# Moving the q and k transposes from TensorE to crossbar DMA, with VectorE copies from SBUF

## The chip, the cores and the metric

The kernel runs on one core of one Trainium2 chip. The metric is the device time of that core in microseconds (us); lower is better. Executions of one kernel mostly lie within 1% of each other; where they scatter more, the text says so. A run counts as slow when it is over 1.5% above the fastest of the same kernel.

Five engines work side by side: PE (TensorE, matmul), DVE (VectorE), ACT (ScalarE), POOL (GpSimd) and SP (SyncE, which here only issues DMAs). Each works through its own list of instructions in a fixed order and stops at the first one whose input is not there (below, VectorE stands 10.43 us before one copy while the input of a later one is ready).

## The reference, cut to what matters

Attention over 8 batches of 8 heads (576 positions, head size 64) with a bias made of running sums, then a mixer: a low-rank mix along the sequence, and a channel mix 512 → 2048 → 512.

```python
cum = np.cumsum(np.maximum(s, 0.0), axis=-1)
bias = -(cum[:, :, :, None] - cum[:, :, None, :])
scores = np.where(causal, -1e9, scale * q @ k.T + np.minimum(bias, 0.0))
attn = softmax(scores);  x = (attn @ v)            # 8 x 576 x 512 after the heads are joined
u = x + (x.T @ U @ V).T                            # sequence mix
out = u + np.maximum(u @ w_ch1, 0.0) @ w_ch2       # channel mix
```

## The kernel before

Heads are handled two at a time: 32 head pairs, numbered n, four to a batch. The score matmuls of this kernel take q and k with the head dimension on the partitions, so each pair's q and k are transposed and copied into one of five "slots" (pair n uses slot n % 5). The transposes run on PE, 16 a pair, into PSUM; VectorE (ScalarE for a few early ones) copies PSUM to the slot.

```python
    def transposes(n):
        b, hp = divmod(n, PB)
        slot = slots[n % NSLOT]
        # ... SP fetches the four bias rows of the slot (cut)
        for hh in range(2):
            h = 2 * hp + hh
            tp = pwork().bitcast(BF16)[:, : 2 * 4 * TP].rearrange("p (c t m) -> p c t m", c=2, t=4)
            for c, src in enumerate((q_t[b], k_t[b])):
                for t2 in range(4):
                    nc.tensor.transpose(
                        tp[:, c, t2, :], src[:, h, ds(t2 * 128, 128)], identity[:TP, :TP]
                    )
            dst = slot[0:D, hh, 0 : 2 * S].rearrange("p (c m t two) -> p c m t two", c=2, t=4, two=2)
            for par in range(2):
                copy = nc.scalar.copy if n == 0 or (b == 1 and par) else nc.vector.tensor_copy
                copy(
                    dst[:, :, :, :, par],
                    tp[par * D : par * D + D].rearrange("p c t m -> p c m t"),
                )
            yield
```

The main loop runs two batches' loads ahead and fills the gaps of the attention with channel-mix matmuls of earlier groups (`step_fill`, inside `run`):

```python
    load(2)
    # ... (cut)
    for n in range(PB, NP + 2):
        b, hp = divmod(n, PB)
        if hp == 0 and 1 < b < B - 1:
            load(b + 1)
        if n + 1 < NP:
            run(transposes(n + 1))
        if n < NP:
            run(scores(n))
        # ... values(n - 1), seqmix(b - 1), chanmix (cut)
    in_program_order(tc, traced, [E.Pool, E.PE])
```

The order of the instructions on each engine is chosen when the kernel is compiled. `in_program_order` adds an edge from each instruction of an engine to the one before it in the program, and so keeps that engine in program order. For the whole program only Pool and PE are held like this. VectorE, ScalarE and SP are held only through batch 0 and are ordered freely by the compiler's scheduler from there on.

The softmax here doesn't subtract the row's maximum and nothing guards it: scores larger than these inputs give would overflow.

## Time and profile before

| | before |
|---|---|
| median time | 404.22 us (3 runs, 404.01 to 404.5) |
| profiled span | 400.4 us, mean granted TensorE clock 0.983 |
| PE busy | 381.6 us (95%) |
| DVE / ACT / POOL busy | 223.8 / 200.5 / 56.6 us |

The page of the kernel before, cut to the busy times and four rows of the picture in 40 slices. A digit is the busy share of a slice (10 us) in tenths; PEclk is the granted TensorE clock in tenths; DMA is the mean busy share of the 16 DMA engines.

```profile
span 400.4 us, 8275 instructions
...
PE 381.6 (95%) x3395; PEld 213.8 (53%) x3395; DVE 223.8 (56%) x473; ACT 200.5 (50%) x384; POOL 56.6 (14%) x79
...
PE   7798989989999899999999999999999999999995
...
DVE  7775036777567866776676756775668252002011
...
PEclk9759999999999999999999999999999999999999
DMA  5999999994596299319951792240154015301002
```

PE is busy 80% or more in every slice from the third to the 39th (most digits are 9), and VectorE has slack in every slice. DMA is full in slices 2 to 9: batch 2's q and k are loaded there, behind weights and the loads of earlier batches.

What does a PE transpose cost? The timeline of PE in the kernel before, around 198 us (columns: start, duration, engine, line, operation, tiles, shapes, count).

```profile
197.94 1.03 PE L432 MATMUL pwork<-uT,w_sb 128*128 128x512 bf16 x4
198.81 0.29 PE L237 MATMUL pwork<-identity,q_sd 72*128 72x72 bf16 x4
198.94 0.29 PE L237 MATMUL pwork<-identity,k_sd 72*128 72x72 bf16 x4
199.07 1.03 PE L432 MATMUL pwork<-uT,w_sb 128*128 128x512 bf16 x4
```

The eight transposes of one head start at 198.81 and the next matmul starts at 199.07, so a group of eight costs 0.26 us of PE's time, two groups 0.52 us a pair. The durations overlap and must not be added.

The groups by shape of VectorE in the kernel before: one slot's copies out of PSUM, and the one cast from SBUF to SBUF of the same shape (busy us, mean ns of one, idle time before).

```profile
L243 DVE COPY slot_93<-pwork 64x576 bf16<-64x576 bf16 x26 | 20.7, 798 | 2.2 <-PE pwork L237 1.9
...
L159 DVE CAST hT<-hT 64x576 bf16<-64x576 f32 x1 | 0.5, 453 | 0.0
```

### The profile page before, as it was taken

The numbers are of one execution on the slowest core, as the hardware profiler recorded it, in microseconds if no ns is written. First come the engines' busy times: TensorE is split into PE (matmuls) and PEld (weight loads), VectorE is DVE, ScalarE is ACT, GpSimd is POOL, SyncE is SP. The second block draws the span as 40 slices with busy tenths as digits, with TensorE's granted clock in tenths as the row PEclk, the third lists the DMA queues.
The fourth block names the chain that finished last, engine by engine and source line by source line (L and its number), as shares of the span: only waits on it lengthen the run. The fifth ranks groups of instructions, "written<-read, shape, count | busy, mean of one in ns | idle before, by whom it ended". The sixth has DMA issues, their size and how long they took to land.

```text
span 400.4 us, 8275 instructions
## 1 busy us (share of the span) xinstructions
PE 381.6 (95%) x3395; PEld 213.8 (53%) x3395; DVE 223.8 (56%) x473; ACT 200.5 (50%) x384; POOL 56.6 (14%) x79
## 2 busy tenths in 40 slices
PE   7798989989999899999999999999999999999995
PEld 2475446645655455555554566555555554444442
DVE  7775036777567866776676756775668252002011
ACT  5552578735753477336743584348533920630610
POOL 5760052300500050005000500000000000000000
PEclk9759999999999999999999999999999999999999
DMA  5999999994596299319951792240154015301002
GB/s 76 160 213 207 166 121 141 137 146 85 82 133 86 67 148 120 55 56 175 114 67 57 141 145 54 72 97 18 38 77 97 16 34 133 79 26 71 10 26 79
DMA packets 94148, 38.31 MB, mean 96 GB/s; under 512 B 77150, under 2 KB 88446, under 8 KB 94110
## 3 DMA queue, kind: packets, MB, share of 16 engines
q0 software_dynamic: 53360, 18.44, 57.5%
q1 hardware_dynamic: 40750, 19.35, 24.1%
q8 instruction: 26, 0.43, 0.5%
q14 instruction: 12, 0.10, 0.1%
HBM read 37.51 MB, written 9.95 MB: 119 GB/s over the span
## 4 chain that ended last, share of the span: by engine, by line
PE 76%; DMA 11%; DVE 6%; ACT 3%; issue 1%; POOL 1%; DVEq 0%; ACTq 0%
PE pwork L444 28%; PE pwork L432 28%; PE pscore L258 8%; DMA k_sd<-in_k_dram 8%; PE pwork L321 6%; PE pwork L237 3%; DMA v_slot_102<-in_v_dram 2%; PE pwork L349 2%; PE pwork L385 2%; DVE slot_96 L243 1%; DVE slot_95 L243 1%; DMA hT<-in_s_dram 1%; DVE x_sb L331 1%; DVE ux L357 1%; DVE o_sb L454 1%
## 5 line engine op out<-in xcount | busy, mean ns | idle before, releaser
L439 ACT ACTIVATE hT<-pwork 128x512 bf16<-128x512 f32 x144 | 88.0, 611 | 112.5 <-PE pwork L432 111.6
L444 PE MATMUL pwork<-w_sb,hT 128*128 128x512 bf16 x576 | 141.3, 379 | 0.2 <-ACT slot_96 L243 0.2
L432 PE MATMUL pwork<-uT,w_sb 128*128 128x512 bf16 x576 | 141.0, 379 | 0.4 <-ACT slot_96 L243 0.3
L444 PEld LDWEIGHTS <-hT 128*128 128x128 bf16 x576 | 52.3, 98 | 50.1 <-issue 0.3
L432 PEld LDWEIGHTS <-w_sb 128*128 128x128 bf16 x576 | 51.0, 98 | 46.9 <-issue 0.4
L454 DVE TENSOR_TENSOR o_sb<-pwork,u_sd 128x512 f32<-128x512 f32 x36 | 24.9, 692 | 63.4 <-PE pwork L444 62.2
L269 ACT ACTIVATE pT_87<-pscore 128x512 bf16<-128x512 f32 x32 | 19.3, 604 | 28.3 <-PE pscore L258 28.2
L331 DVE TENSOR_TENSOR x_sb<-pwork,rec 128x320 bf16<-128x320 f32 x64 | 31.3, 490 | 2.0
L98 POOL DMA_DIRECT2D q_sd<-in_q_dram x10 | 8.3, 829 | 148.6 <-PE pwork L237 132.5
L269 ACT ACTIVATE pT_86<-pscore 128x512 bf16<-128x512 f32 x32 | 19.3, 604 | 18.5 <-PE pscore L258 18.4
L243 DVE COPY slot_96<-pwork 64x576 bf16<-64x576 bf16 x22 | 17.4, 797 | 13.8 <-PE pwork L237 13.5
L270 DVE TENSOR_TENSOR pT_86<-pT_86,keep 128x512 bf16<-128x512 bf16 x32 | 13.2, 414 | 21.1 <-ACT pT_86 L269 21.0
L330 DVE RECIPROCAL rec<-pwork 128x5 f32<-128x5 f32 x64 | 12.1, 191 | 20.8 <-PE pwork L321 20.7
L367 DVE TENSOR_TENSOR uT<-pwork,xT 128x256 bf16<-128x256 f32 (+6 forms) x54 | 19.8, 418 | 6.1 <-PE pwork L385 6.1
L270 DVE TENSOR_TENSOR pT_87<-pT_87,keep 128x512 bf16<-128x512 bf16 x32 | 13.2, 417 | 17.5 <-ACT pT_87 L269 17.4
L237 PEld LDWEIGHTS <-q_sd 72*128 72x128 bf16 x256 | 15.9, 100 | 12.8 <-DMA q_sd<-in_q_dram 1.6
L237 PE MATMUL pwork<-identity,k_sd 72*128 72x72 bf16 x256 | 19.1, 201 | 2.9 <-DMA k_sd<-in_k_dram 2.8
L243 DVE COPY slot_93<-pwork 64x576 bf16<-64x576 bf16 x26 | 20.7, 798 | 2.2 <-PE pwork L237 1.9
L282 ACT ACTIVATE pT_87<-pscore 128x512 bf16<-128x512 f32 x32 | 19.5, 610 | 4.6 <-PE pscore L258 4.5
L282 ACT ACTIVATE pT_86<-pscore 128x512 bf16<-128x512 f32 x32 | 19.5, 609 | 4.5 <-PE pscore L258 4.5
L321 PEld LDWEIGHTS <-pT_87 128*128 128x128 bf16 x480 | 18.6, 99 | 5.8 <-DVE pT_87 L295 0.4
L321 PEld LDWEIGHTS <-pT_86 128*128 128x128 bf16 x480 | 18.4, 100 | 4.8 <-DVE uT L367 0.5
(96 smaller groups left out, 434.1 us busy)
## 6 DMA issues: line engine op xcount, KB each, us to landing
out_dram<-o_sb SPq DMA_DIRECT2D x36, 256.0 KB
w_sb<-in_moe_w_ch_dram POOLq DMA_DIRECT2D x2, 2048.0 KB, 20.6
q_sd<-in_q_dram POOLq DMA_DIRECT2D x7, 576.0 KB, 8.1
k_sd<-in_k_dram POOLq DMA_DIRECT2D x7, 576.0 KB, 14.0
v_slot_102<-in_v_dram POOLq DMA_DIRECT2D x12, 128.0 KB, 14.3
v_slot_103<-in_v_dram POOLq DMA_DIRECT2D x12, 128.0 KB, 14.7
v_slot_104<-in_v_dram POOLq DMA_DIRECT2D x8, 128.0 KB, 16.9
rows_hbm<-hT SPq DMA_DIRECT2D x1, 504.0 KB
```

What stands on the lines that cost most here:

```text
L237: nc.tensor.transpose(tp[:, c, t2, :], src[:, h, ds(t2 * 128, 128)], identity[:TP, :TP])
L243: copy(dst[:, :, :, :, par], tp[par * D : par * D + D].rearrange("p c t m -> p c m t"),)
L258: nc.tensor.matmul(dst, lhsT=kT[:, ds(j * 128, 128)], rhs=qT[:, lo:hi], start=True, stop=True,)
L269: nc.scalar.activation(pT[:, hh, 0:512], diag, EXP, scale=scale)
L270: nc.vector.tensor_tensor(pT[:, hh, 0:512].rearrange("p (a b) -> p a b", a=4), pT[:, hh, 0:512].rearrange("p (a b) -> p a b", a=4), keep.t ...
L282: nc.scalar.activation(pT[:, hh, 512:1024], far, EXP, scale=scale)
L321: nc.tensor.matmul(po[:, i, :], lhsT=pT[:, hh, ds(place(j, i), 128)], rhs=vt[:, j, h, :], start=(j == 0), stop=(j == i), skip_group_check= ...
L331: nc.vector.tensor_tensor(x_sb[:, hp, :, ds(hh * D, D)], po[:, :, 0:D], rec.to_broadcast([128, 5, D]), op=ALU.mult,)
L432: nc.tensor.matmul(f1, lhsT=w1_sb[:, kt, ds(nf * 128, 128)], rhs=u[:, kt, :], start=(kt == 0), stop=(kt == 3),)
L439: nc.scalar.activation(hT[:, nf, :], f1, RELU)
L444: nc.tensor.matmul(f2, lhsT=hT[:, nf, ds(i * 128, 128)], rhs=w2_sb[:, nf, :], start=(nf == 0), stop=(nf == NF - 1),)
L454: nc.vector.tensor_tensor(o_sb.rearrange("p (a b) -> p a b", a=4), f2.rearrange("p (a b) -> p a b", a=4), u_sd[:, :, i, :], op=ALU.add,)
```

## The change

The intent: PE is the limit, so take work off PE. For the pairs from 8 on (batches 2 to 7) a DMA that transposes in the crossbar writes q and k of a pair, transposed, to SBUF. VectorE copies from there to the slot. The loads now share one tile `qk` of 80 rows (72 used) per batch, two tiles in turn; Pool clears rows 64 to 79 before the first load that is read by the crossbar.

```diff
+    TR = 80
+    qks = [consts.tile([TR, H, 2, TT * D], BF16, name=f"qk{i}") for i in range(2)]
 ...
+    def fetch(n):
+        b, hp = divmod(n, PB)
+        qkT_of[n] = work.tile([128, 2, 2, 4, TR], BF16, tag="qkT", name="qkT")
+        nc.sync.dma_start_transpose(
+            out=qkT_of[n].rearrange("p a c t m -> p (a c t) m"),
+            in_=qks[b % 2][:, ds(2 * hp, 2), :, :].rearrange("p h c x -> p (h c x)"),
+        )
 
     def transposes(n):
 ...
+        qkT = qkT_of.pop(n, None)
         for hh in range(2):
+            if qkT is not None:
+                tp = qkT[:, hh, :, :, :TP]
+            else:
+                tp = pwork()...          # the eight PE transposes as before (cut)
 ...
     def load(b):
-        alloc_qk(b)
+        if b < FT + 2:
+            nc.gpsimd.memset(qks[b % 2][64:, :, :, :], 0.0)
         load_qk(b, 0, H)
 ...
+        if FT * PB <= n + 2 < NP:
+            fetch(n + 2)
         if n + 1 < NP:
             run(transposes(n + 1))
```

More of the change, by code (lines that the diff above doesn't have):

```diff
@@ L71 @@
     consts = ctx.enter_context(tc.tile_pool(name="consts", bufs=1))
-    loads = ctx.enter_context(tc.tile_pool(name="loads", bufs=2))
     work = ctx.enter_context(tc.tile_pool(name="work", bufs=2))
@@ L88 @@
     nc.sync.dma_start(out=s_sb, in_=s.rearrange("b h s -> (b h) s"))
-    q_t, k_t = {}, {}
-    def alloc_qk(b):
-        q_t[b] = loads.tile([TP, H, TT * D], BF16, tag="q_sd", name="q_sd")
-        k_t[b] = loads.tile([TP, H, TT * D], BF16, tag="k_sd", name="k_sd")
+    TR = 80
+    qks = [consts.tile([TR, H, 2, TT * D], BF16, name=f"qk{i}") for i in range(2)]
     def load_qk(b, h, n):
-        for dst, src in ((q_t[b], q), (k_t[b], k)):
+        for c, src in enumerate((q, k)):
             nc.gpsimd.dma_start(
-                out=dst[:, ds(h, n), :],
+                out=qks[b % 2][:TP, ds(h, n), c, :],
                 in_=src[b, ds(h, n)].rearrange("h (p t) d -> p h (t d)", p=TP),
             )
-    alloc_qk(0)
     load_qk(0, 0, 2)
@@ L168 @@
             )
-    for dst in (q_t[0], k_t[0]):
-        nc.vector.memset(dst[:, 4:8, 0:2], 0.0)
+    nc.vector.memset(qks[0][:TP, 4:8, :, 0:2], 0.0)
     load_qk(0, 4, 4)
@@ L208 @@
     nc.gpsimd.dma_start(out=w2_sb, in_=moe_w_ch2.rearrange("(kt kp) n -> kp kt n", kp=128))
-    alloc_qk(1)
     load_qk(1, 0, H)
     load_v(1)
-    uT_of, x_of, xT_of = {}, {}, {}
+    uT_of, x_of, xT_of, qkT_of = {}, {}, {}, {}
     def uT(g):
@@ L229, in transposes @@
             )
+        qkT = qkT_of.pop(n, None)
         for hh in range(2):
             h = 2 * hp + hh
-            tp = pwork().bitcast(BF16)[:, : 2 * 4 * TP].rearrange(
-                "p (c t m) -> p c t m", c=2, t=4
-            )
-            for c, src in enumerate((q_t[b], k_t[b])):
-                for t2 in range(4):
-                    nc.tensor.transpose(
-                        tp[:, c, t2, :], src[:, h, ds(t2 * 128, 128)], identity[:TP, :TP]
-                    )
+            if qkT is not None:
+                tp = qkT[:, hh, :, :, :TP]
+            else:
+                tp = pwork().bitcast(BF16)[:, : 2 * 4 * TP].rearrange(
+                    "p (c t m) -> p c t m", c=2, t=4
+                )
+                for c in range(2):
+                    for t2 in range(4):
+                        nc.tensor.transpose(
+                            tp[:, c, t2, :],
+                            qks[b % 2][:TP, h, c, ds(t2 * 128, 128)],
+                            identity[:TP, :TP],
+                        )
             dst = slot[0:D, hh, 0 : 2 * S].rearrange("p (c m t two) -> p c m t two", c=2, t=4, two=2)
```

## The prediction

> **What bounds the kernel now.** TensorE. The page gives PE 95% busy over a 400.4 us span. The table by 10 us windows shows PE busy 10.00 of 10 us in nearly every window from 90 us on, at a granted clock of 1.00. The chain of waits is 76% PE. VectorE (56%) and ScalarE (50%) are not limits there. Before 90 us it is different: DMA is saturated (DMA row 9 in slices 2 to 9, PE 44.3 of 49 us busy between 41 and 90 us), and the chain runs through the batch-1 k load (22.8 to 53.8 us).
>
> **What the change removes.** The 16 PE transposes per head pair for 24 of 32 pairs: 384 of 512. [...] The timeline shows the true cost: at 198.81 us a group of eight starts, at 199.07 us the next matmul: 0.26 us. Two groups per pair, 24 pairs: 48 x 0.26 = 12.5 us of PE issue time, nearly all in the stretch where PE never waits, so on the critical path.
>
> **What it moves.** 96 VectorE copies, 798 ns each from PSUM, now read SBUF. [...] a 64x576 cast within SBUF took 453 ns. I estimate about 450 ns, some 33 us less VectorE time, off the critical path.
>
> **What it adds.** 24 crossbar transposes of 80x2048 (about 328 KB) on SP's queue. The 128x640 one (164 KB) took 1.2 us on SP's queue and about 0.9 us of the 16 DMA engines near 209 us; twice the bytes gives an estimate of 1.7 us of the engines, landing about 3.5 us after issue. Fetches go two pairs ahead (8.9 us a pair), so hidden. Two memsets of 16 x 8192 on Pool: from 64x520 in 527 ns, an estimated 8 us each, before loads 2 and 3. The first falls partly into Pool's idle time (34.6 to 46.0 us).
>
> **The danger** is 45 to 100 us. Load 2 was issued at 46 and 51 us and took almost 20 us to land. A copy no longer follows a PE instruction in program order; it depends only on a DMA. VectorE and SP run in a fixed order chosen at compile time: SP issued pair 8's row load at 31 us already. If the copies of pair 8 are placed among those of pairs 4 to 7, VectorE blocks until load 2 and its transpose land (about 75 us) and PE stalls; this could cost 5 to 18 us.
>
> **Sum.** 404.2 - 12.5 = 391.7, plus an expected 2.3 us for stalls at the start of batches 2 and 3: 394.0 us; 80% range 389.0 to 407.0. Faster by over 2%: 0.60; within 2%: 0.28; slower by over 2%: 0.12.
>
> **What would show it right.** PE transposes 128 left; PE matmul starts between 100 and 320 us stay gapless, and a head pair takes about 8.35 instead of 8.87 us; slot copies from SBUF near 450 ns; DVE busy falls by 30 us; qkT transposes 1.2 to 2 us on SP's queue after 100 us; the end of batch 1 (about 93 us) does not move. Wrong: VectorE or TensorE idle "until DMA qkT"; SP waiting on q/k loads with the first u_sd or xT transposes behind it; slot copies still near 800 ns.
>
> **What would make it wrong.** VectorE blocked by an early-placed copy; an 80-row transpose that [...] takes several times my estimate; late xT transposes behind qkT ones.

The sum is 404.2 − 12.5 + 2.3 = 394.0 us. The 450 ns for a copy rest on one cast of the same shape (453 ns): an estimate.

## The result, and the profile after

| | before | after |
|---|---|---|
| median time | 404.36 us (4 runs, 404.01 to 404.89) | 427.44 us (4 runs, 426.01 to 428.72) |
| profiled span, granted clock | 400.4 us, 0.983 | 425.2 us, 0.940 |

The kernel became slower: ratio 1.0569, 95% interval 1.0530 to 1.0607. Here and below a ratio is the mean time of one kernel's fast runs over that of the other's of the same rounds, so not quite the ratio of the medians that are quoted.

The page after, the same rows as shown of before.

```profile
span 425.2 us, 7532 instructions
...
PE 372.5 (88%) x2961; PEld 204.1 (48%) x3011; DVE 208.7 (49%) x472; ACT 200.6 (47%) x384; POOL 70.8 (17%) x81
...
PE   7798983457159998999999989999999999999996
...
DVE  7665051719076577665855775676435435101001
...
PEclk9769998597569999999999999999999999999999
DMA  5999999999989939985996993446212614401001
```

PE has less to do than before, as intended, yet from the seventh to the twelfth slice its row reads 345715 where it read 998999 before. The clock row shows dips in the same place. From the thirteenth slice on everything is as before or better.

To see it by stage, take the stretches between the first matmuls of successive sequence mixes (one per batch), read from the PE timelines:

| stretch (sequence mix of batch) | 0→1 | 1→2 | 2→3 | 3→4 | 4→5 | 5→6 | 6→7 |
|---|---|---|---|---|---|---|---|
| before, us | 51.0 | 47.2 | 39.7 | 41.5 | 42.0 | 41.1 | 26.7 |
| after, us | 71.1 | 59.6 | 38.2 | 39.9 | 39.9 | 39.0 | 26.2 |
| difference | +20.1 | +12.4 | −1.5 | −1.6 | −2.1 | −2.1 | −0.5 |

The gain is there: 2.1 us for a batch, which is four pairs at 0.52 us. The first two stretches lose 32.5 us, and the gains return 7.8.

What happens in them? The VectorE timeline after, from 60 to 136 us, the three lines with a long wait. The bracket gives the idle time before an instruction and what ended it.

```profile
76.55 0.82 DVE L251 COPY slot_92<-qkT 64x576 bf16<-64x576 bf16 x1 [10.43 <-DMA qkT<-qk_69]
...
95.68 0.65 DVE L251 COPY slot_89<-qkT 64x576 bf16<-64x576 bf16 x1 [7.94 <-DMA qkT<-qk_69]
...
119.03 1.96 DVE L251 COPY slot_91<-qkT 64x576 bf16<-64x576 bf16 x3 [12.09 <-DMA qkT<-qk_70]
```

VectorE stands still three times, 30.5 us in all, each time at a slot copy whose crossbar transpose has not landed. The slots are those of pairs 8, 10 and 12. PE stands still in turn. Its timeline after, the four long waits:

```profile
79.75 0.61 PE L452 MATMUL pwork<-w_sb,hT 128*128 128x512 bf16 x1 [11.69 <-DVE x_sb L339]
...
96.78 0.99 PE L329 MATMUL pwork<-v_slot_100,pT_83 128*128 128x65 bf16 x15 [5.43 <-DVE x_sb L339]
...
106.99 1.37 PE L357 MATMUL pwork<-x_sb,U_sb 128*128 128x512 bf16 x5 [2.03 <-DVE x_sb L339]
...
122.04 1.91 PE L452 MATMUL pwork<-w_sb,hT 128*128 128x512 bf16 x4 [13.26 <-DVE ux L365]
```

PE never waits for a copy of pair 8, 10 or 12. It waits for `x_sb` and `ux`: other work of VectorE, for earlier pairs, that stands behind the blocked copy in VectorE's list. The four waits are 32.4 us.

Why does it stand behind? Two lines of the same VectorE timeline, after the first stall. Pair 8 uses slot_92 here (its first copy, at 76.55, is shown above), pair 7 slot_91.

```profile
79.22 0.47 DVE L339 TENSOR_TENSOR x_sb<-pwork,rec 128x320 bf16<-128x320 f32 x1
...
79.72 0.75 DVE L251 COPY slot_91<-pwork 64x576 bf16<-64x576 bf16 x1
```

Pair 8's first copy comes before pair 7's, although the PE transposes of pair 7 had ended at 68.07, and before the work on `x_sb` that PE waits for until 79.75. In the kernel before, pair 7's copies begin at 67.91 and pair 8's at 73.97. There a slot copy needs the output of a PE transpose, and PE is held in program order, so the copy could not be ready early. Now it needs only a DMA, and the scheduler, which seems to have taken that DMA to be done soon, put it early.

When was that DMA done? SP's queue after: the crossbar transposes of pairs 8/9, 10/11 and 12/13, and one late in the run. SP's line shows the time that the issue took.

```profile
69.88 5.51 SPq L219 DMA_TRANSPOSE qkT<-qk_69  x2
...
82.25 9.18 SPq L219 DMA_TRANSPOSE qkT<-qk_69  x2
...
105.77 8.54 SPq L219 DMA_TRANSPOSE qkT<-qk_70  x2
...
277.33 1.34 SPq L219 DMA_TRANSPOSE qkT<-qk_70  x1
```

Pair 8's transpose could be issued only at 69.88, when batch 2's k load (issued at 50.93) had landed. It landed by 76.5. Pair 10's took 13.4 us from its issue at 82.25 to 95.66, while load 3 was under way. At 277 us, where the DMA row of the page stands at 4 of 10, one issue takes 1.34 us.

This stall cost more than its length. The table of windows of the kernel after (columns: window, its length, then busy us and instructions of PE, PEld, DVE, ACT and POOL; the last three are granted clock, DMA share and GB/s; this share counts the whole time of every packet that starts in the window, so it can pass 1).

```profile
69.00:72.00 3.00, 0.00 (x0) 0.00 (x0) 0.00 (x0) 0.00 (x0) 3.00 (x1) 0.74 2.78 90
72.00:75.00 3.00, 0.00 (x0) 0.00 (x0) 0.00 (x0) 0.00 (x0) 3.00 (x1) 0.50 1.18 35
...
81.00:84.00 3.00, 3.00 (x13) 1.39 (x12) 2.38 (x5) 1.72 (x3) 0.26 (x1) 0.50 1.13 145
84.00:87.00 3.00, 2.95 (x48) 2.24 (x48) 2.47 (x6) 2.45 (x5) 0.00 (x0) 0.99 2.43 158
```

From 81 to 84 us PE is busy all the time, but at half the clock: four 128x512 matmuls take 1.90 us there (timeline at 81.93) and 1.03 us at 84.29. (The counts x13 and x48 are of different shapes.) In finer windows the clock fell to half at 70.4 us (hence the mean of 0.74), 2.4 us after PE's last matmul had ended at 68.07, and was back at 84.1 us, 4.3 us after PE set in again at 79.75.

The slot copies after, from the groups by shape, for a slot where waits are few:

```profile
L251 DVE COPY slot_93<-qkT 64x576 bf16<-64x576 bf16 x20 | 13.2, 658 | 2.3 <-PE pscore L266 2.1
```

They take 658 ns, against 798 before and about 450 expected.

### The profile page after: what moved, and what is told of

The parts are those of the page before. It is cut to its first block, busy times and chain, and to the rows that moved or that the text cites. A ratio compares the mean times of both kernels' runs of the same rounds, so it can differ in the third digit from the quotient of the medians.

```text
span 425.2 us, 7532 instructions
## 1 busy us (share of the span) xinstructions
PE 372.5 (88%) x2961; PEld 204.1 (48%) x3011; DVE 208.7 (49%) x472; ACT 200.6 (47%) x384; POOL 70.8 (17%) x81
## 3 DMA queue, kind: packets, MB, share of 16 engines
q0 software_dynamic: 53360, 18.44, 48.5%
## 4 chain that ended last, share of the span: by engine, by line
PE 66%; DMA 22%; DVE 8%; issue 2%; SPq 1%; POOL 1%; ACT 0%; DVEq 0%; ACTq 0%
PE pwork L440 26%; PE pwork L452 25%; PE pscore L266 7%; DMA qk_70<-in_q_dram 7%; PE pwork L329 5%; DMA qkT<-qk_69 5%; DMA qk_69<-in_k_dram 4%; DMA qkT<-qk_70 3%; DMA v_slot_99<-in_v_dram 2%; DVE slot_92 L251 2%; PE pwork L393 1%; SPq L219 1%; DVE slot_90 L251 1%; DVE o_sb L462 1%; PE pwork L357 1%
## 5 line engine op out<-in xcount | busy, mean ns | idle before, releaser
L440 PE MATMUL pwork<-uT,w_sb 128*128 128x512 bf16 x551 | 135.5, 379 | 2.2 <-DVE uT L379 0.4
L452 PEld LDWEIGHTS <-hT 128*128 128x128 bf16 x576 | 54.3, 99 | 68.0 <-DVE x_sb L339 11.8
L440 PEld LDWEIGHTS <-w_sb 128*128 128x128 bf16 x576 | 52.4, 98 | 52.7 <-issue 1.1
L277 ACT ACTIVATE pT_84<-pscore 128x512 bf16<-128x512 f32 x32 | 19.3, 604 | 25.1 <-PE pscore L266 25.0
L277 ACT ACTIVATE pT_83<-pscore 128x512 bf16<-128x512 f32 x32 | 19.3, 603 | 23.5 <-PE pscore L266 23.5
L278 DVE TENSOR_TENSOR pT_84<-pT_84,keep 128x512 bf16<-128x512 bf16 x32 | 13.4, 419 | 24.6 <-ACT pT_84 L277 24.5
L375 DVE TENSOR_TENSOR uT<-pwork,xT 128x256 bf16<-128x256 f32 (+6 forms) x54 | 19.7, 416 | 6.2 <-PE pwork L393 5.7
L290 ACT ACTIVATE pT_83<-pscore 128x512 bf16<-128x512 f32 x32 | 19.5, 608 | 5.9 <-PE pscore L266 5.9
L290 ACT ACTIVATE pT_84<-pscore 128x512 bf16<-128x512 f32 x32 | 19.5, 611 | 4.5 <-PE pscore L266 4.5
L251 DVE COPY slot_92<-qkT 64x576 bf16<-64x576 bf16 x20 | 13.4, 671 | 13.3 <-DMA qkT<-qk_69 10.4
L294 ACT ACTIVATE pT_84<-pscore 128x512 bf16<-128x512 f32 x32 | 19.7, 616 | 0.0
L294 ACT ACTIVATE pT_83<-pscore 128x512 bf16<-128x512 f32 x32 | 19.7, 614 | 0.0
L251 DVE COPY slot_89<-qkT 64x576 bf16<-64x576 bf16 x20 | 13.1, 657 | 11.7 <-DMA qkT<-qk_69 7.9
L146 PE MATMUL pscore<-busy 128*128 128x512 bf16 (+1 forms) x51 | 17.4, 433 | 1.3 <-DVE busy L122 1.3
L251 DVE COPY slot_91<-qkT 64x576 bf16<-64x576 bf16 x16 | 10.6, 662 | 15.1 <-DMA qkT<-qk_70 12.1
## 6 DMA issues: line engine op xcount, KB each, us to landing
qk_69<-in_q_dram POOLq DMA_DIRECT2D x3, 576.0 KB, 12.5
```

The lines of the kernel that those rows point to most:

```text
L251: copy(dst[:, :, :, :, par], tp[par * D : par * D + D].rearrange("p c t m -> p c m t"),)
L277: nc.scalar.activation(pT[:, hh, 0:512], diag, EXP, scale=scale)
L278: nc.vector.tensor_tensor(pT[:, hh, 0:512].rearrange("p (a b) -> p a b", a=4), pT[:, hh, 0:512].rearrange("p (a b) -> p a b", a=4), keep.t ...
L290: nc.scalar.activation(pT[:, hh, 512:1024], far, EXP, scale=scale)
L294: nc.scalar.activation(pT[:, hh, 1024:1536], mid, EXP, scale=scale)
L440: nc.tensor.matmul(f1, lhsT=w1_sb[:, kt, ds(nf * 128, 128)], rhs=u[:, kt, :], start=(kt == 0), stop=(kt == 3),)
```

## The experiments

The theory to test (A): the transposes themselves pay as predicted; all of the loss comes from VectorE's freely chosen order, which puts DMA-fed copies ahead of ready work. The rivals: (B) the crossbar traffic slows the loads and the other DMAs, and with them everything; (C) the crossbar data is simply too late in batches 2 and 3, in whatever order VectorE works; (D) the Pool memsets delay the loads. The recorded expectations letter the rivals otherwise: their B (run 1) is C here, their C (runs 3 and 4) is B and D here, their D (run 5) is that only an order fixed throughout helps, and E and F (run 9) are about the time of load 3. Twelve kernels ran, all correct against the reference. The medians are of four runs each, unless slow ones are left out; "before" in the same rounds had a median of 402.1 to 403.7 us.

### 1. VectorE held in program order

```diff
-    in_program_order(tc, traced, [E.Pool, E.PE])
+    in_program_order(tc, traced, [E.Pool, E.PE, E.DVE])
```

> The kernel after, with VectorE kept in program order (one engine added to the list of the last ordering call); same instructions. Theory A (VectorE's fixed order puts the slot copies of pairs 8, 10 and 12 ahead of other pairs' work, and it blocks there until their loads and transposes land): the three VectorE waits of 10.4, 7.9 and 12.1 us shrink to at most 3 us each, PE no longer idles 11.7 and 13.3 us, 392 to 399 us. Rival B (the q/k data of batches 2 and 3 come too late whatever the order): the waits move to PE before the score matmuls of pairs 8 and 12 and the time stays at 418 us or more.

Measured: 394.33 us (392.93 to 394.91), ratio to before 0.9796 [0.9761, 0.9831]. One edit to the order alone takes 33 us off. The stretches are 52.7, 47.2, 37.6, 39.5, 39.9, 39.0, 26.2: both lost stretches are back near the values of before. The transposes on SP's queue still run (5.77 us for pairs 8/9, issued at 69.87). So the order is what makes the loss; B, C and D may still cost something in what is left: VectorE still waits 4.75 us for crossbar data at 118.93 us and 5.06 us at 164.33, more than the 3 us expected, but PE has no wait over 1.5 us behind these.

### 2. The same on the kernel before

The same edit on the kernel before the change, as a control: if program order were better in itself, run 1 would say little.

> Control: the kernel before, with VectorE kept in program order. Both theories: 402 to 406 us, because there each copy follows PE transposes that are in program order already. If it gains several us by itself, then what e1 gains is not all due to the copies of the change.

Measured: 407.82 us, ratio 1.0141 [1.0101, 1.0181], a little above the expected 402 to 406. Holding VectorE costs the old kernel 1.4%, in the first two stretches (54.4 and 48.5, against 51.0 and 47.2). So the free order was the better choice before the change and a bad one after it.

### 3. The crossbar traffic alone

PE transposes are kept for all pairs, the crossbar transposes run too, and nobody reads them.

```diff
-        qkT = qkT_of.pop(n, None)
+        qkT_of.pop(n, None)
+        qkT = None
```

> The kernel after with all its loads, memsets and 24 crossbar transposes, whose results nobody uses: the PE transposes of before feed the copies in all batches. Theory A and B: 403 to 407 us, the added traffic is harmless while nobody waits for it. Rival C (the traffic or the Pool memset itself delays other work): 412 us or more.

Measured: 414.99 us, ratio 1.0308 [1.0243, 1.0374]. The expectation, 403 to 407, was missed. All of it is in the second stretch (59.0 against 47.2). The VectorE timeline of this run, and then SP's queue in this run:

```profile
128.88 0.69 DVE L463 TENSOR_TENSOR o_sb<-pwork,u_sd 128x512 f32<-128x512 f32 x1 [8.45 <-DMA u_sd<-uT]
```

```profile
93.77 9.06 SPq L219 DMA_TRANSPOSE qkT<-qk  x2
...
103.89 2.17 SPq L219 DMA_TRANSPOSE qkT<-qk  x1
...
106.70 3.57 SPq L219 DMA_TRANSPOSE qkT<-qk  x1
...
111.08 9.82 SPq L435 DMA_TRANSPOSE u_sd<-uT  x1
```

SP's queue in the kernel before, the same transpose:

```profile
93.49 2.17 SPq L426 DMA_TRANSPOSE u_sd<-uT  x1
```

The transpose that the channel mix needs was issued at 111 instead of 93 us, because SP first sat in four new ones, and it was slow itself (9.82 us against 2.17). It is the same kind of fault on another list: SP too is ordered freely. So B is right in part: where SP's list is unlucky, the new transposes hold up others. How much of the 3.1% is the list and how much the traffic, this run doesn't separate.

### 4. Crossbar from batch 4 on

If C held, moving the whole change to batches 4 to 7, when DMA is much quieter, would cure it.

```diff
-        if b < FT + 2:
+        if FT + 2 <= b < FT + 4:
             nc.gpsimd.memset(qks[b % 2][64:, :, :, :], 0.0)
 ...
-        if FT * PB <= n + 2 < NP:
+        if 16 <= n + 2 < NP:
```

> The kernel after with the crossbar route only from batch 4 on (16 of 32 pairs), where loads are issued long ahead. Theories A and B: no stall of VectorE on a qkT transpose; the gain is 16 pairs x 0.52 us = 8.3 us of PE, so 395 to 398 us. If the steady part of the change has a cost of its own (the kernel after gained 10.2 us, not 12.5, after batch 1), 397 to 400 us. Rival C: above 404 us.

Measured: 428.14 us, ratio 1.0647 [1.0608, 1.0685]; the expectation, 395 to 398, was missed by 30 us. The stretches are 50.7, 57.8, 61.8, then 39.9, 39.9, 39.0, 26.2. VectorE's two longest waits in this run:

```profile
129.05 0.65 DVE L251 COPY slot<-qkT 64x576 bf16<-64x576 bf16 x1 [6.13 <-DMA qkT<-qk]
...
191.44 2.63 DVE L251 COPY slot<-qkT 64x576 bf16<-64x576 bf16 x4 [16.24 <-DMA qkT<-qk]
```

The stalls moved along with the change: the first is at pair 16, the first crossbar pair, the second at pair 20, the first of the next batch. So the crowded start of the kernel alone was not to blame. The order is not the whole of this run either: pair 20's transpose could be issued only at 175.22 us, when load 5 had landed, and load 5 had waited for the second memset, which this edit moved too (154.33 to 161.25 us). How much of the 16.24 us is owed to that is not separated.

### 5. Only the DMA-fed copies are tied

Only what the change let loose is held: each copy from `qkT` gets an edge to the VectorE instruction before it in the program. All else stays free.

```diff
+                if qkT is not None:
+                    tied.append(len(nc.cur_bb.bb.instructions))
                 copy(dst[:, :, :, :, par], ...)
 ...
     in_program_order(tc, traced, [E.Pool, E.PE])
+    after_previous(tc, tied, E.DVE)      # one edge per copy, no semaphore
```

> The kernel after, with only the slot copies held to their place on VectorE (each copy that reads a crossbar result follows the VectorE instruction traced before it); everything else stays free to move. Theory A: no early block, as in e1 (2.0% under before), without the cost that keeping all of VectorE in order had in the control e2 (1.4%): ratio to before 0.965 to 0.980, 389 to 396 us at a before of 404. Rival D (only an order fixed throughout helps): 410 us or more.

Measured: 392.3 and 395.57 us in the two fast runs (mean 393.9), ratio 0.9775 [0.9710, 0.9840]. The other two, 399.51 and 402.68 us, count as slow (granted clock 0.968 and 0.969, against 0.978 and 0.974) and are left out; with them the median is 397.54. The profile is of the fastest. Its stretches are 52.7, 46.0, 37.6, 39.4, 39.9, 39.0, 26.2. SP's queue and the first crossbar copy of pair 8:

```profile
68.98 5.86 SPq L234 DMA_TRANSPOSE qkT<-qk  x2
```

```profile
75.81 3.18 DVE L268 COPY slot<-qkT 64x576 bf16<-64x576 bf16 x4 [0.28 <-DMA qkT<-qk]
```

The transpose was issued and landed about when it did in the kernel after. The wait for it fell from 10.43 to 0.28 us, since VectorE had other work before it. This is the plainest proof of A. The scatter of the runs is not explained, and the ratio rests on two runs alone.

### 6. Tied copies, first memset moved early

D says that the memset ahead of load 3 holds that load back. So it goes to the start of the program, before load 1 (the same buffer).

```diff
+    nc.gpsimd.memset(qks[1][64:, :, :, :], 0.0)
     load_qk(1, 0, H)
 ...
-        if b < FT + 2:
+        if b == FT:
             nc.gpsimd.memset(qks[b % 2][64:, :, :, :], 0.0)
```

> e5 with the Pool memset of the second q/k buffer moved ahead of its first load (batch 1), so load 3 is issued near 68 us rather than near 75 us. If load 3's lateness still costs something in e5: 1 to 5 us under e5. If not: within 1 us of e5. The cost would be load 1 issued up to 7 us later (21.5 to 28 us), which could stall PE at 53 us by a few us.

Measured: 412.69 us (one of the four runs slow; the mean of the three fast ones is 411.8), ratio 1.0219 [1.0161, 1.0278]: 18 us slower than the fast runs of run 5, where a gain of 1 to 5 us or no change was expected. SP's queue and the copy of pair 8 in this run:

```profile
68.75 16.36 SPq L235 DMA_TRANSPOSE qkT<-qk  x2
```

```profile
87.88 2.67 DVE L269 COPY slot<-qkT 64x576 bf16<-64x576 bf16 x4 [12.92 <-DMA qkT<-qk]
```

Load 3 was issued at 68.24 instead of 76.09 us, just ahead of the crossbar transposes of pairs 8 and 9. The same two took 16.36 us of SP's queue instead of 5.86, with the copy 12 us later. Beside each other, the load issued by Pool and the transposes issued by SP both got slower (the q and k of load 3 took 13.6 and 19.7 us to land, against 10.4 and 12.6 in run 5). Load 1 went out later too (27.20 instead of 21.34 us), but that is not the reason: load 2 landed at 68.7 us here and at 68.9 in run 5. The 6.92 us memset ahead of load 3, which looked like a pure cost, had kept the load out of the transposes' way by chance. D falls for this memset, with its sign turned round. And C holds in part: with the order tied, late crossbar data still cost, for PE now waits 9.73 us for the slot copy itself. The first stretch is 65.1 us against 52.7 in run 5. The rest is in the third (46.0 against 37.6), where VectorE waits 5.88 us for an `xT` transpose that SP issued at 141.82 us, just after a load at 140.38.

### 7. The memset move alone, in free order

The same move on the kernel after, with nothing tied.

> The kernel after with only that memset moved; VectorE's order free. Theory A: the block at pair 12 (12.1 us) shrinks by up to 7 us, those at pairs 8 and 10 stay; 417 to 424 us. If the lateness of load 3 was the whole of the second loss, the stretch between the second and third sequence mix falls from 59.6 to about 47 us.

Measured: 427.3 us, ratio 1.0609 [1.0553, 1.0665], the same as the kernel after; 417 to 424 was expected. Pair 8's wait grew to 15.45 us (until 88.08), as in run 6, and the free order lost on top. This agrees with run 6 on the memset, and with A that the order must be mended first.

### 8. Copies in the order of their source

Run 6, with the copies walking the source contiguously and writing the slot with strides.

```diff
-                    dst[:, :, :, :, par],
-                    tp[par * D : par * D + D].rearrange("p c t m -> p c m t"),
+                    dst[:, :, :, :, par].rearrange("p c m t -> p c t m"),
+                    tp[par * D : par * D + D],
```

> e6 with each slot copy from SBUF walked in the order of the source (72 contiguous elements innermost) rather than of the destination. The copies took 658 ns, not the 450 ns estimated. [...] about 450 ns now. If not: 640 to 680 ns again. Time within 1 us of e6 either way, VectorE being off the critical path.

Measured: 420.59 us, ratio 1.0440 [1.0397, 1.0484]. The group of these copies in this run:

```profile
L275 DVE COPY slot<-qkT 64x576 bf16<-64x576 bf16 x96 | 139.9, 1457 | 15.8 <-DMA qkT<-qk 14.8
```

1457 ns instead of some 660: both expectations (450, or no change) were missed, and so was that the time stays within 1 us of run 6. In these runs the order in which the elements were walked mattered more (1457 against 658 ns) than where they lay (658 ns from SBUF against 798 from PSUM). Why, no run here settles. In the steady stretches the time rose, too (41.7 against 39.9 in 4→5), so slack of VectorE is not without end: its busy time was 282.6 us here.

### 9. Load 3 still later

If load 3 out of the way is good, later might be better: run 5 with the memset ahead of load 3 done twice.

```diff
-            nc.gpsimd.memset(qks[b % 2][64:, :, :, :], 0.0)
+            for _ in range(b - 1):
+                nc.gpsimd.memset(qks[b % 2][64:, :, :, :], 0.0)
```

> e5 with the Pool memset ahead of load 3 done twice, so load 3 is issued about 7 us later (near 83 us instead of 76). Theory E (the first crossbar transposes are slow because load 3 is queued on the same DMA engines; e6, with load 3 near 68 us, had the first result at 87.9 us instead of about 76): the transposes of pairs 10 and 11 take no longer than in e5, no wait at pair 8, and the time stays at or under e5, 388 to 397 us, with less scatter than e5's 392 to 403; a wait of up to 8 us for pair 12 is possible. Rival F (e6 was slow from its later load 1 or another order): later load 3 only costs, 400 us or more.

Measured: 400.37 us, ratio 0.9933 [0.9904, 0.9961]; the expectation was missed. The load went out at 82.23, and met the transposes of pairs 10 and 11 instead (4.45 and 6.32 us on SP's queue, against 3.42 and 5.04 in run 5). And the experiment carried a cost of its own. Pool's memsets and one VectorE copy of this run; then the same pair in run 4, where it can be seen too:

```profile
68.04 13.89 POOL L535 MEMSET qk<- 16x8192 bf16 x2 [5.50 <-PE pwork L258]
```

```profile
78.38 3.96 DVE L268 COPY slot<-qkT 64x576 bf16<-64x576 bf16 x1 [3.67 <-DMA qkT<-qk]
```

```profile
154.33 6.92 POOL L517 MEMSET qk<- 16x8192 bf16 x1 [38.16 <-PE pwork L243]
```

```profile
156.73 4.92 DVE L251 COPY slot<-qkT 64x576 bf16<-64x576 bf16 x1
```

The two copies, of a kind that takes 0.65 us otherwise, ended at 82.34 and 161.65; the memsets beside them ended at 81.93 and 161.25. Each copy ended 0.4 us after the memset. A mask with two SBUF inputs, in the same memset of run 9, was not held:

```profile
72.70 0.42 DVE L295 TENSOR_TENSOR pT<-pT,keep 128x512 bf16<-128x512 bf16 x1 [2.00 <-ACT pT L294]
```

So two copies from SBUF were held to the end of a memset, and the mask took 0.42 us beside one. Moving a copy's source from PSUM to SBUF thus brought a new neighbour in these two runs. Copies of the same shape from PSUM, beside the same memsets, were not held: 0.79 us at 69.07 us in run 9, and four in 3.26 us at 153.18 us in run 4. Why the ones are held and the others not, no run shows. The run doesn't separate this cost from that of the later load. Its 400.37 us is what rival F named (400 us or more), but F's reason, the later load 1 of run 6, does not hold (see there).

### 10. Tied copies, crossbar from pair 12 on

Leave the crowded time to PE: run 5 with batch 2 (pairs 8 to 11) on PE transposes again.

```diff
-        if FT * PB <= n + 2 < NP:
+        if 12 <= n + 2 < NP:
```

> e5 with the crossbar route only from pair 12 (batch 3) on, so no transpose runs while loads 2 and 3 fill the DMA queues. Gain at most 20 pairs x 0.52 us = 10.4 us. Theories A with E: no VectorE wait on a crossbar result over 3 us before 140 us, ratio to before 0.970 to 0.980 (392 to 396 us), scatter under 3 us. If the first pairs of any late start are slow, as in e4 (VectorE waits of 6.1 and 16.2 us there): above 400 us.

Measured: 392.37 us (391.08 to 393.5), ratio 0.9741 [0.9716, 0.9767], the lowest ratio of all and the only one that is faster by over 2% clear of noise; run 5's two fast runs can't be told from it. 20 pairs at 0.52 us are 10.4 us; the medians differ by 10.25. The stretches are 50.7, 45.7, 37.6, 39.4, 39.9, 39.0, 26.2. VectorE waits for crossbar data 7.6 us in all, 3.6 us at most, and PE has no wait over 1.5 us between 55 and 150 us. The page:

```profile
span 389.4 us, 7639 instructions
...
PE 368.5 (95%) x3025; PEld 203.9 (52%) x3075; DVE 212.4 (55%) x472; ACT 200.6 (52%) x384; POOL 71.0 (18%) x81
...
PE   7798998989999899999998999999999999999996
```

PE's row is full throughout, as before the change, with 13.1 us less busy time (somewhat too much: the trace lacks 50 matmul records, x3025 against x3075 weight loads).

### 11. Tied copies, load 2 before the v load of batch 1

The other way to have batch 2 in time: run 5 with its q and k loaded earlier.

```diff
     load_qk(1, 0, H)
-    load_v(1)
 ...
         load_qk(b, 0, H)
+        if b == 2:
+            load_v(1)
         load_v(b)
```

> e5 with load 2's q and k issued before the v load of batch 1, so they are issued near 34 to 40 us rather than 45 and 50 us and should land by about 60 us, before load 3 is issued. Theory A with E: the first crossbar transposes are issued by about 62 us and land before pair 8 needs them; all 24 pairs pay: ratio to before 0.962 to 0.974 (388 to 393 us), scatter under 4 us. If batch 1's v now comes late, PE waits near 66 us for it, and the gain is lost.

Measured: 394.94 us, ratio 0.9802 [0.9781, 0.9822]; 0.962 to 0.974 was expected. Load 2 went out near 31 us and pair 8's copies found their data. But batch 1's v came later, and PE waited for it (0.67, 1.01 and 0.27 us near 67 to 69 us, and 2.73 at the mix); the first stretch is 54.0. The DMA engines moved about as much before 90 us as in run 5 (149 and 152 GB/s on average), so what one load gains another loses.

### 12. Crossbar from pair 12, in free order

The last corner: the later start of run 10 without its ties.

> The kernel after with the crossbar route only from pair 12 on, and VectorE's order left free (e10 without the tie). If late data alone was the fault, the order is harmless once the first transposes come late enough: 391 to 395 us, as e10. If the free order is a fault of its own (e4, free from pair 16, blocked for 6.1 and 16.2 us), VectorE waits over 4 us on crossbar results remain and the time is above 398 us.

Measured: 419.77 us, ratio 1.0413 [1.0372, 1.0454]. VectorE's two longest waits in this run:

```profile
94.52 0.65 DVE L251 COPY slot<-qkT 64x576 bf16<-64x576 bf16 x1 [7.62 <-DMA qkT<-qk]
...
142.74 0.65 DVE L251 COPY slot<-qkT 64x576 bf16<-64x576 bf16 x1 [21.56 <-DMA qkT<-qk]
```

The chain of waits of this run, at the second of them (start, duration, what):

```profile
126.25 16.40 DMA qkT<-qk
```

This is pair 16, the first of batch 4. Its transpose could be issued only when load 4 had landed (126.06 us), and took 16.4 us beside load 5 (issued at 120.95 and 122.07 us), and VectorE stood before it from early on. The four corners (medians, us; of run 5 the fast runs alone, with slow ones 397.5):

| | crossbar from pair 8 | from pair 12 |
|---|---|---|
| free order | 427.4 | 419.8 |
| copies tied | 393.9 | 392.4 |

The ties are worth 27 to 34 us. The later start is worth 8 us in the free order; with the ties its 1.5 us lie within the scatter of run 5. The order of VectorE is the cause; the crowded DMA decides how long each blocked copy waits.

## Why the prediction was wrong

- **The size of the gain was right.** The prediction has 0.26 us for a group of eight. The runs gave 2.1 us a batch and, in run 10, 10.25 us for 20 pairs. A pair takes 8.34 to 8.39 us in the steady part of the kernel after, within a batch; 8.35 was predicted.
- **The danger was named and mis-sized.** This is the step that failed: "plus an expected 2.3 us for stalls at the start of batches 2 and 3". The prediction saw that pair 8's copies, if placed among those of pairs 4 to 7, would block VectorE, "this could cost 5 to 18 us", but in the sum it entered with 2.3 us. The copies were placed early not once but for pairs 8, 10 and 12, and the two stretches lost 32.5 us. Run 1 gave nearly all of it back with one edit to the order. The term should have been some 30 us, or the order should have been settled before giving odds.
- **It took the landing from a quiet moment.** "Landing about 3.5 us after issue" came from a transpose near 209 us. With loads queued on the DMA engines the landing took 6.6 us (pair 8), 13.4 us (pair 10) and 16.4 us (run 12). "Fetches go two pairs ahead, so hidden" failed in that part of the run, and held later (1.34 us of SP's queue at 277 us; VectorE's last wait for crossbar data in the kernel after ends at 123.08 us).
- **The clock was left out.** After the four long waits PE ran at half clock: from 79.75 to 84.1, from 96.78 to 101.1, from 107.9 to 108.8 and from 122.04 to 125.0 us. In the two stretches PE's idle time rose from 4.8 to 36.2 us, which is 31.4 of the 32.5 us lost. Its busy time rose too, by 1.1 us, although transposes had been taken from it: some 12.1 us of it were at half clock, which cost about 6 us (an estimate: half of that time).
- **The copies.** 658 ns, not 450, so VectorE's busy time fell by 15.1 us and not 30. The copies did get quicker, 658 ns against 798, but this walk of the elements is not the one of the cast that the estimate used (453 ns). It was off the critical path and cost nothing.
- **"The end of batch 1 does not move"** was wrong: its sequence mix began at 107.0 us instead of 86.3.
- **The memset** was estimated at 8 us and took 6.92; that it would help by delaying load 3 nobody had foreseen.

What stays open: why the copies take 658 ns, and 1457 in the other order; the scatter of run 5; how the 3.1% of run 3 divides; what the moved memset cost in run 4; and that the scheduler believed the DMA to be early is inferred from the order that it made.

## What to carry to other kernels

When work moves from a compute engine to a DMA, the instructions that used to follow that engine lose their place: ask of every consumer which edge now keeps it from being put early in its own engine's list, and give it one back if there is none. Take a DMA's latency from the stage in which it will run, with that stage's loads queued, and not from a quiet one (here 6.6 to 16.4 us, against the 3.5 expected); give the data time where the DMA engines are full (run 10), but settle the order first, since in the free order a later start did not cure it (runs 4 and 12). If an in-order engine waits at an instruction for a later pair while another engine waits for an earlier pair's result, it is the order that is wrong, not the throughput.
